# Eight LayerNorm tiles transposed by DMA in 16-bit halves instead of on TensorE

## The chip, the cores and the metric

One core of one Trainium2 chip. The metric is the device time of one execution in microseconds. A core has TensorE (PE, matmuls, results in PSUM), VectorE (DVE), ScalarE (ACT), GpSimd (POOL), and SyncE (SP), whose queue issues nearly all DMA transfers of this kernel. Each engine works through its own instructions in order; semaphores order the engines among themselves.

## The reference

A transformer block with adaptive LayerNorm: 2048 rows of 512 values, attention with 32 query heads over 8 cached key/value heads (the last 512 cached positions), and a gated feed-forward of width 1792.

```python
x = A_x
mod = (_silu(c) @ w_mod).reshape(c.shape[0], 6, 1, -1)
sa, ca, ga, sb, cb, gb = (mod[:, 0], mod[:, 1], mod[:, 2], mod[:, 3], mod[:, 4], mod[:, 5])
h = _layernorm(x, axis=-1) * (1 + ca) + sa
x = x + ga * _A_ref(h, A_k_cache, A_v_cache, A_wq, A_wo)   # softmax(q k^T / sqrt(128)) v, then wo
h = _layernorm(x, axis=-1) * (1 + cb) + sb                 # the second LayerNorm
x = x + gb * _B_ref(h, B_w_gate, B_w_up, B_w_down)         # (gelu(h wg) * (h wu)) wd
```

All tensors are float32. The kernel keeps precision by splitting each operand in two 16-bit halves, a high part and the remainder (a *pair*), and makes each product of three matmuls: low x high, high x high, high x low (`mm3`).

## The kernel before

**The stages.** The attention runs over 128 *units*: two halves of the rows (first 1024, last 1024), in each half 16 pairs of heads, in each pair two heads times two blocks of 512 rows. A unit is four *slots*; slot `t` handles 128 rows of one head: scores on PE (`ps`), row maximum on DVE (`nm`, L982), exponential on ACT (`ee`, L991), the high half of the probabilities on ACT two slots later (`p`, L1003), the low half on DVE three slots later (L1008), and then one DMA transpose of both halves (`pt`, L1012). The product of probabilities and values (`po`) of a unit is made two units later. Its results (`ot` pairs) wait for the output projection (`py`), which runs tile by tile over the next eight units, once four heads are there, and adds into `acc`, the residual rows. The scores have two PSUM banks, in turn; the other PSUM tiles share five under the tag `acc`.

**The order of the work** is written out by hand. In every slot the code issues the scores, the maximum, the delayed steps, then up to three product groups of `mm3` from a list (`pop()`: query projection, `py`, `po`), then whatever is registered for this slot: `at(t, fn)`, then the loads that fall due, and last `at(("w", t), fn)`. `spare` moves background transfers into slots that have no other.

**The second LayerNorm of the first 1024 rows.** When the last addition to a row tile of 128 rows is made (`attn_final`), `ln_tile(2, ...)` returns seven steps that are registered 1, 5, 8, 9, 10, 12 and 13 slots later: `stat` (mean and variance on DVE, a power on POOL), `norm` (POOL, in place in `acc`), `turn` (four transposes of 128x128 on PE against the identity, into a PSUM tile `pln`), two affine steps (ACT, `hf<-pln,cols`, after the second the result is written to DRAM as `hs`), and two steps that split the result into the pair blocks of the feed-forward stage (ACT high, POOL low). Twelve slots later the tile of `acc` is loaded with rows of the second half. There are eight such tiles, `ti` 0 to 7, around the change from the first to the second half of the attention. The tiles of `ln_tile(1, ...)`, the first LayerNorm of the last 1024 rows, use the same `turn` earlier on. The second LayerNorm of the last 1024 rows (`ln_turned`) already turns its tiles by DMA, in the feed-forward stage.

**In the same stretch** the modulation columns are made (`mod_col`, L137, which reads `sbc`, a tile of the tag `ot`), and the feed-forward weights begin to be prepared (`prep_set`), through tiles of the tag `raw` (`stage`), which five buffers serve and from which `hf` is taken too.

**The feed-forward stage** multiplies by a seven-product scheme (Strassen-like): from four blocks 11, 12, 21, 22 of the gated activations four combinations t1, t3, t2, t4 are made (`sums_of`), and all are kept as pairs `at`. For five passes of seven the down projection uses them (`turned(n)`), in the order of products 1, 2, 6, 5, 7, 3, 4; product 5 reads t1, 7 reads t3, 6 reads t2, 4 reads t4. The pairs `at` share the tag `ot` with the attention outputs.

Of the kernel before, what the change touches and what calls it, by code (L numbers as in the profile page):

```python
# [11 lines left out]
F16 = mybir.dt.float16  # L12
U16 = mybir.dt.uint16
BF16 = mybir.dt.bfloat16
AF = mybir.ActivationFunctionType
ALU = mybir.AluOpType
# [23 lines left out]
GU = 2.0 ** -38  # L40
PRE = 2.0 ** -20
TINY = 1e-36
NOT = 12
LDGAP = 1
NRAW = 5
NRW = 2
# [18 lines left out]
def block_kernel(ctx: ExitStack, tc: tile.TileContext, x, kT, v, wq, wo, wg, wu, wd, cT, wc, wm, out):  # L65
# [8 lines left out]
    def tmp(name):  # L74
        return pool.tile([P, 512], F32, tag="e", name=name, bufs=NE)

    def raw(name):
        return pool.tile([P, 512], F32, tag="raw", name=name, bufs=NRAW)
# [397 lines left out]
    def ln_tile(gen, i, src):  # L476
        jsc, jsh = ln_cols("a" if gen < 2 else "f")
        qb, i = divmod(i % (2 * QT), QT)
        st = {}

        def load():
            if gen == 2:
                st["x"] = src()
            else:
                st["x"] = raw("xs")
                dma(st["x"], src())

        def stat():
            ln_stat(st["x"], st)
            ln_power(st)  # L490

        def norm():
            if gen == 2:
                return pool_ts(st["x"], st["x"], st["mv"][:, 0:1], st["rs"], ALU.subtract, ALU.mult)
            nc.vector.tensor_scalar(st["x"], st["x"], st["mv"][:, 0:1], st["rs"], op0=ALU.subtract, op1=ALU.mult)

        def turn():
            st["ps"] = bank("acc", "pln", NACC)
            for dt in range(KT):
                nc.tensor.transpose(st["ps"][:, dt * P:(dt + 1) * P], st["x"][:, dt * P:(dt + 1) * P], ident)  # L500

        def affine(dts):
            if 0 in dts:
                st["f"] = raw("hf") if gen == 2 else tmp("hf")
            f = st["f"]
            for dt in dts:
                sl = slice(dt * P, (dt + 1) * P)
                nc.scalar.activation(f[:, sl], st["ps"][:, sl], AF.Identity,
                                     scale=cols[:, jsc, dt:dt + 1], bias=cols[:, jsh, dt:dt + 1])
            if KT - 1 in dts:  # L510
                dma(spilled(gen, qb)[:, :, i * P:(i + 1) * P], f.rearrange("p (k q) -> p k q", k=KT))

        def parts(act):
            o = slice(i * P, (i + 1) * P)
            f = st["f"].rearrange("p (k q) -> p k q", k=KT)
            for h, name in enumerate(("b11", "b21") if qb == 0 else (None, "b22")):
                if name:
                    t, src = block(gen, name), f[:, 2 * h:2 * h + 2, :]
                    if act:
                        nc.scalar.activation(t[:, 0:2, o], src, AF.Copy)  # L520
                    else:
                        nc.gpsimd.tensor_tensor(t[:, 2:4, o], src, t[:, 0:2, o], op=ALU.subtract)

        more = [lambda: parts(True), lambda: parts(False)]
        return load, [stat, norm, turn, lambda: affine((0, 1)), lambda: affine((2, 3))] + more

    TURN = {}

# [429 lines left out]
    def attn_final(ti):  # L958
        y1[ti] = dram.tile([P, D], F32, name=f"y{ti}")
        dma(y1[ti], acc[ti])  # L960
        if ti < 2 * QT:
            nxt = ti + 2 * QT
            own, steps = ln_tile(2, ti, lambda: acc[ti])
            own()
            for d, fn in zip((1, 5, 8, 9, 10, 12, 13), steps):
                at(("w", now[0] + d), fn)
            at(now[0] + 12, lambda: load_acc(nxt, rows_of(x, nxt)))
        else:
            ln_last(ti - 2 * QT)
# [294 lines left out]
    def f_items(q, hold=None):  # L1264
        n, m = divmod(q, 2)
        st = {}
        done = set()

        def add(k, src):
            nc.vector.tensor_tensor(st[k], st[k], st[src], op=ALU.add)  # L1270

        def gelu(key, src):

            def apply():
                dst = tmp("fg") if key == "21" else src
                nc.scalar.activation(dst, src, AF.Gelu_apprx_tanh, scale=col("finv", f_scale(q)))
                G[n, key] = dst

            return (apply,)

        def result(key, src):
            if m == 0:
                for step in gelu(key, src):
                    step()
            else:
                g = G[n, key]
                nc.vector.scalar_tensor_tensor(g, g, col("gsc", n % NP), src, op0=ALU.mult, op1=ALU.mult)  # L1287
                if not turned(n):
                    parts(key, G.pop((n, key)), nc.vector)
                elif key != "12":  # L1290
                    parts(key, g, nc.vector)
                else:
                    sums_of()

        def parts(key, g, eng):
            t = A[n, key] = pair("ot", "at", NOT)
            nc.scalar.activation(t[:, 0, :], g, AF.Copy)  # L1297
            eng.tensor_tensor(t[:, 1, :], g, t[:, 0, :], op=ALU.subtract)

        def sums_of():  # L1300
            g = {k: G.pop((n, k)) for k in ("11", "12", "21", "22")}
            for o, a, b in (("11", "12", "11"), ("12", "22", "12"), ("22", "22", "11"), ("21", "21", "22")):
                nc.gpsimd.tensor_tensor(g[o], g[a], g[b], op=ALU.subtract)  # L1303
                parts({"11": "t1", "12": "t3", "22": "t2", "21": "t4"}[o], g[o], nc.gpsimd)

        def out_(key, src):
            if not hold:
                result(key, src)
            else:
                hold.append(gelu(key, src))  # L1310

        def place(k):
            if m == 0:
                return pool.tile([P, QB], F32, tag="k", name="fg", bufs=2) if k == 6 else tmp("fg")
            return pool.tile([P, QB], F32, tag="p16", name="fu", bufs=NP16) if k == "s1" else kept(k)

        def after(k):
            done.add(k)
            if k in (1, 6, 7):
                name = {1: "s1", 6: "u2", 7: "u3"}[k]  # L1320
                keep(st, name, place(name))
            if k == 2:
                add("s1", "b")
                out_("11", st["s1"])
            elif k == 4:
                out_("21", st["a"])
            elif k == 3:
                add("u2", "c")
                out_("12", st["u2"])
            if k in (5, 7) and {5, 7} <= done:  # L1330
                add("u3", "c")
                out_("22", st["u3"])

        tags = {"a": ("s", "fa", 2) if q else ("qa", "fa", 1), "b": ("acc", "fb", NACC), "c": ("acc", "fc", NACC)}
        return with_posts(("f", q), 2 + q // (2 * NP), banks(st, tags), after)
# [448 lines left out]
```

## Time and profile before

| what | value |
|---|---|
| three runs | 1743.76, 1745.96, 1745.58 us; median 1745.58 |
| profiled execution | 1743.57 us, with a span of 1741.8 us |
| granted TensorE clock | 1.0 |
| busy: PE, DVE, ACT, POOL | 1714.7, 1417.6, 1258.5, 1045.9 us |
| DMA | 339.82 MB, mean 195 GB/s |

The span is the time from the first to the last instruction of the profiled execution. Busy time is what the profiler saw an engine work; a share of it is an average over stages with different limits. In a row of the timeline the first number is the start in us from the span's start, the second the length; the releaser in brackets is what ended the engine's idle time by the semaphores of the profile, and where an instruction waits for several, it may name the wrong one. In a row of a group the numbers behind the bar are busy us and mean ns of one; in a row of one tile or source line the three numbers are the shortest, median and longest in ns.

### The profile page before, as it was taken

Reading aid. Unit: us, or ns where it says so; the run is one execution under the profiler, and the core shown is the slowest. Engines: PE = TensorE matmul, PEld = TensorE weight load, DVE = VectorE, ACT = ScalarE, POOL = GpSimd, SP = SyncE. Lnnn points to the kernel's source line nnn. Section 1 sums busy time; section 2 is a strip of 40 time slices with the busy share of each in tenths; the row PEclk is TensorE's granted clock in tenths of the full one; section 3 lists DMA queues with packets and bytes.
Section 4 is the critical chain, followed back from the end, with each engine's and each line's share of the span. In section 5 each row is a group of like instructions: output and inputs, shape, how many; then the busy total and the mean of one; then the engine's idle time right before and its main releaser. Section 6 shows DMA issues by size and latency. Waiting matters only on the chain.

```text
span 1741.8 us, 26188 instructions
## 1 busy us (share of the span) xinstructions
PE 1714.7 (98%) x8022; PEld 787.0 (45%) x8022; DVE 1417.6 (81%) x2454; ACT 1258.5 (72%) x2813; POOL 1045.9 (60%) x1266
## 2 busy tenths in 40 slices
PE   7999999999999999999999999999999999999998
PEld 5444444444444444444444444444444444444443
DVE  7898898888888899888888788888886678556674
ACT  6988788888878777898778778787784554643344
POOL 4889778776788884654675665754621558313422
PEclk9999999999999999999999999999999999999999
DMA  7999999999999999999999999899986663743235
GB/s 236 218 205 211 213 214 207 223 206 221 215 217 228 205 205 187 212 213 230 201 219 224 208 223 220 186 235 218 197 180 150 187 177 128 191 139 100 91 97 167
DMA packets 690636, 339.82 MB, mean 195 GB/s; under 512 B 578880, under 2 KB 601408, under 8 KB 690496
## 3 DMA queue, kind: packets, MB, share of 16 engines
q1 hardware_dynamic: 690208, 337.63, 85.5%
q8 instruction: 63, 1.03, 0.3%
q14 instruction: 77, 0.63, 0.1%
q10 hardware_dynamic: 288, 0.52, 0.1%
HBM read 135.66 MB, written 61.87 MB: 113 GB/s over the span
## 4 chain that ended last, share of the span: by engine, by line
PE 82%; ACT 5%; DVE 5%; DMA 3%; POOL 2%; issue 2%; SPq 0%; ACTq 0%; DVEq 0%; POOLq 0%
PE py L90 19%; PE ps L90 17%; PE po L90 17%; PE qa L90 8%; PE fa L90 6%; PE qc L90 4%; PE fc L90 3%; PE ya L90 2%; PE qb L90 2%; PE fb L90 2%; PE yc L90 1%; ACT ee L991 1%; DMA yv<-yu 1%; ACT p L1003 1%; DVE nm L982 1%
## 5 line engine op out<-in xcount | busy, mean ns | idle before, releaser
L991 ACT ACTIVATE ee<-ps,nm 128x512 f32<-128x512 f32 x512 | 350.1, 684 | 191.9 <-DVE nm L982 189.3
L1008 DVE SCALAR_TENSOR_TENSOR p<-ee,rr,p 128x512 f16<-128x512 f32 x512 | 460.0, 898 | 4.5 <-ACT p L1003 3.9
L982 DVE TENSOR_REDUCE nm<-ps 128x1 f32<-128x512 f32 x512 | 350.4, 684 | 106.1 <-PE ps L90 103.2
L90 PE MATMUL ps<-k,qt 128*128 128x512 f16 x1536 | 414.9, 379 | 5.6 <-ACT ee L991 4.4
L1003 ACT ACTIVATE p<-ee,rr 128x512 f16<-128x512 f32 x512 | 364.6, 712 | 19.0 <-DVE rr L999 10.0
L90 PE MATMUL po<-pt,v 128*128 128x512 f16 x1536 | 373.0, 379 | 2.7 <-DVE kmax L183 1.4
L90 PE MATMUL py<-wo,ot 128*128 128x512 f16 x1536 | 371.5, 379 | 0.1
L90 PEld LDWEIGHTS <-w 128*128 128x128 f16 x2184 | 213.3, 98 | 263.3 <-issue 4.7
L90 PEld LDWEIGHTS <-v 128*128 128x128 f16 x1536 | 149.9, 98 | 184.9 <-DMA pt<-p 2.3
L90 PEld LDWEIGHTS <-ot 128*128 128x128 f16 x1536 | 150.3, 98 | 181.7 <-DVE ot L740 0.5
L90 PEld LDWEIGHTS <-qt 128*128 128x128 f16 x1536 | 145.9, 98 | 176.9 <-issue 4.7
L1303 POOL TENSOR_TENSOR fg<-fg 128x512 f32<-128x512 f32 x40 | 51.8, 1295 | 135.6 <-DVE fg L1287 103.0
L740 DVE SCALAR_TENSOR_TENSOR ot<-po,ot 128x512 f16<-128x512 f32 x128 | 87.7, 685 | 39.1 <-ACT ot L739 38.6
L1297 ACT ACTIVATE at<-fg 128x512 f16<-128x512 f32 x86 | 53.4, 625 | 64.8 <-DVE fg L1287 44.5
L991 ACT ACTIVATION_READ_ACCUMULATOR ee<-ps,nm 128x1 f32 x512 | 99.9, 195 | 0.0
L952 DVE SCALAR_TENSOR_TENSOR acc<-py,ysc,acc 128x512 f32<-128x512 f32 x128 | 94.7, 740 | 6.2 <-PE py L90 6.2
L235 POOL TENSOR_TENSOR lw<-lw,half__86 128x1 f32<-128x1 f32 x37 | 23.4, 633 | 104.2 <-DVE lw L185 104.1
L90 PE MATMUL fa<-t,w 128*128 128x512 f16 x336 | 83.6, 379 | 1.9 <-ACT u L885 1.4
L90 PE MATMUL qa<-t,w 128*128 128x512 f16 x348 | 84.9, 379 | 0.0
L397 POOL TENSOR_TENSOR rs<-rs,nhalf 128x1 f32<-128x1 f32 x32 | 18.8, 586 | 103.6 <-DVE rs L391 100.7
L739 ACT ACTIVATE ot<-po 128x512 f16<-128x512 f32 x128 | 73.8, 577 | 5.0 <-PE po L90 5.0
L1657 DVE SCALAR_TENSOR_TENSOR yt<-ya,dyc,yt 128x512 f32<-128x512 f32 x68 | 50.1, 745 | 22.1 <-PE ya L90 21.7
(241 smaller groups left out, 2794.0 us busy)
## 6 DMA issues: line engine op xcount, KB each, us to landing
w<-kept SPq DMA_DIRECT2D x123, 256.0 KB, 3.3
wo<-kept SPq DMA_DIRECT2D x70, 256.0 KB, 3.4
kept<-stage SPq DMA_DIRECT2D x61, 256.0 KB, 3.3
raw<-in_wo SPq DMA_DIRECT2D x56, 256.0 KB, 3.2
kept<-w SPq DMA_DIRECT2D x39, 256.0 KB, 3.4
rw<-in_wq SPq DMA_DIRECT2D x38, 256.0 KB, 3.2
hs<-hf SPq DMA_DIRECT2D x32, 256.0 KB, 2.9
pt<-p SPq DMA_TRANSPOSE x512, 3.5
```

Of the source, the lines that this page charges most:

```text
L90: nc.tensor.matmul(ps, a, b, start=first and n == 0, stop=last and n == 2, skip_group_check=chain)
L235: nc.gpsimd.tensor_tensor(out, out, half_, op=ALU.pow)
L739: nc.scalar.activation(t[:, 0, :], src, AF.Copy, scale=scale)
L740: return lambda: nc.vector.scalar_tensor_tensor(t[:, 1, :], src, scale, t[:, 0, :], op0=ALU.mult, op1=ALU.subtract)
L952: nc.vector.scalar_tensor_tensor(acc[ti], st["p"], by, acc[ti], op0=ALU.mult, op1=ALU.add)
L982: nc.vector.tensor_reduce(nm, E[t]["ps"], axis=AX.X, op=ALU.max, negate=True)
L991: nc.scalar.activation(e, E[t]["ps"], AF.Exp, bias=E[t]["nm"], scale=1.0, accum_out=sm[:, t % 2:t % 2 + 1])
L1003: nc.scalar.activation(p16[:, 0, :], E[t]["e"], AF.Copy, scale=E[t]["r"])
L1008: nc.vector.scalar_tensor_tensor(p16[:, 1, :], E[t]["e"], E[t]["r"], p16[:, 0, :], op0=ALU.mult, op1=ALU.subtract)
L1297: nc.scalar.activation(t[:, 0, :], g, AF.Copy)
L1303: nc.gpsimd.tensor_tensor(g[o], g[a], g[b], op=ALU.subtract)
L1657: nc.vector.scalar_tensor_tensor(YT[key], ps, by, YT[key], op0=ALU.mult, op1=ALU.add)
```

## The change

For the eight tiles of the second LayerNorm of the first 1024 rows, the four PE transposes are replaced by: a copy to the high 16-bit half on ACT (`high`), the remainder on POOL (`low`), one DMA transpose of both halves (`turn_dma`, in SP's queue), and the sum of the two turned halves on DVE into a tile `hf` of the tag `raw` (`joined`). The affine steps then work in place in that tile. The steps stand 1, 5, 8, 9, 12, 16, 18, 19, 21 and 22 slots behind the last addition. The halves take a new tag `lnh` of three buffers, the turned halves `lnt` of two. In the feed-forward stage the combinations t1, t3 and t2 now take `lnh` and t4 takes `lnt`, and the tag `ot` has 10 buffers instead of 12. The tiles of `ln_tile(1, ...)` keep the PE transposes.

```diff
--- before.py
+++ after.py
@@ -40,7 +40,7 @@
 GU = 2.0 ** -38
 PRE = 2.0 ** -20
 TINY = 1e-36
-NOT = 12
+NOT = 10
 LDGAP = 1
 NRAW = 5
 NRW = 2
@@ -499,9 +499,25 @@
             for dt in range(KT):
                 nc.tensor.transpose(st["ps"][:, dt * P:(dt + 1) * P], st["x"][:, dt * P:(dt + 1) * P], ident)
 
+        def high():
+            st["h"] = pair("lnh", "lnh", 3)
+            nc.scalar.activation(st["h"][:, 0, :], st["x"], AF.Copy)
+
+        def low():
+            nc.gpsimd.tensor_tensor(st["h"][:, 1, :], st["x"], st["h"][:, 0, :], op=ALU.subtract)
+
+        def turn_dma():
+            st["t"] = pool.tile([P, 2, KT, P], F16, tag="lnt", name="lnt", bufs=2)
+            nc.sync.dma_start_transpose(st["t"].rearrange("p h k q -> p (h k) q"), st["h"].rearrange("p a b -> p (a b)"))
+
+        def joined():
+            st["f"] = raw("hf")
+            nc.vector.tensor_tensor(st["f"].rearrange("p (k q) -> p k q", k=KT), st["t"][:, 0], st["t"][:, 1], op=ALU.add)
+            st["ps"] = st["f"]
+
         def affine(dts):
-            if 0 in dts:
-                st["f"] = raw("hf") if gen == 2 else tmp("hf")
+            if 0 in dts and gen < 2:
+                st["f"] = tmp("hf")
             f = st["f"]
             for dt in dts:
                 sl = slice(dt * P, (dt + 1) * P)
@@ -522,7 +538,8 @@
                         nc.gpsimd.tensor_tensor(t[:, 2:4, o], src, t[:, 0:2, o], op=ALU.subtract)
 
         more = [lambda: parts(True), lambda: parts(False)]
-        return load, [stat, norm, turn, lambda: affine((0, 1)), lambda: affine((2, 3))] + more
+        turns = [high, low, turn_dma, joined] if gen == 2 else [turn]
+        return load, [stat, norm] + turns + [lambda: affine((0, 1)), lambda: affine((2, 3))] + more
 
     TURN = {}
 
@@ -962,7 +979,7 @@
             nxt = ti + 2 * QT
             own, steps = ln_tile(2, ti, lambda: acc[ti])
             own()
-            for d, fn in zip((1, 5, 8, 9, 10, 12, 13), steps):
+            for d, fn in zip((1, 5, 8, 9, 12, 16, 18, 19, 21, 22), steps):
                 at(("w", now[0] + d), fn)
             at(now[0] + 12, lambda: load_acc(nxt, rows_of(x, nxt)))
         else:
@@ -1293,7 +1310,7 @@
                     sums_of()
 
         def parts(key, g, eng):
-            t = A[n, key] = pair("ot", "at", NOT)
+            t = A[n, key] = pair(*{"t4": ("lnt", "at", 2)}.get(key, ("lnh", "at", 3) if key[0] == "t" else ("ot", "at", NOT)))
             nc.scalar.activation(t[:, 0, :], g, AF.Copy)
             eng.tensor_tensor(t[:, 1, :], g, t[:, 0, :], op=ALU.subtract)
 
```

## The prediction

> **What bounds the kernel now.** I read the page first, for the engine that has no room, then the page's chain that ended last.
>
> ```profile
> span 1741.8 us, 26188 instructions
> PE 1714.7 (98%) x8022; PEld 787.0 (45%) x8022; DVE 1417.6 (81%) x2454; ACT 1258.5 (72%) x2813; POOL 1045.9 (60%) x1266
> PE 82%; ACT 5%; DVE 5%; DMA 3%; POOL 2%; issue 2%; SPq 0%; ACTq 0%; DVEq 0%; POOLq 0%
> ```
>
> TensorE (PE) is busy 98% of the span and carries 82% of the chain. A microsecond taken from PE is a microsecond off the end, unless another engine becomes the limit in that stretch. So the next views are PE's own timeline around the eight turns, and the busy times by stretch there.
>
> ```profile
> L500 PE MATMUL pln<-ident,acc x32: 272/273/300, 700.4 to 775.5; 128*128 128x128 f32 x32
> 699.75 0.81 PE L90 MATMUL po<-pt,v 128*128 128x512 f16 x3
> 700.39 0.60 PE L500 MATMUL pln<-ident,acc 128*128 128x128 f32 x4
> 700.83 0.81 PE L90 MATMUL ps<-k,qt 128*128 128x512 f16 x3
> ...
> 730.84 0.81 PE L90 MATMUL po<-pt,v 128*128 128x512 f16 x3
> 732.28 0.63 PE L500 MATMUL pln<-ident,acc 128*128 128x128 f32 x4 [0.63 <-POOL w L158]
> ...
> 774.02 0.81 PE L90 MATMUL po<-pt,v 128*128 128x512 f16 x3
> 775.15 0.63 PE L500 MATMUL pln<-ident,acc 128*128 128x128 f32 x4 [0.33 <-ACT hf L508]
> ```
>
> ```profile
> 540.00:550.00 10.00, 8.56 (x41) 3.77 (x40) 9.41 (x16) 8.57 (x22) 7.35 (x9) 1.00 1.20 226
> 700.00:780.00 80.00, 79.04 (x385) 37.96 (x384) 69.98 (x134) 69.17 (x172) 45.79 (x50) 1.00 1.00 212
> 720.00:760.00 40.00, 39.37 (x191) 18.74 (x190) 37.74 (x73) 34.25 (x86) 27.13 (x27) 1.00 0.99 213
> 700.00:800.00 100.00, 99.04 (x478) 47.01 (x477) 86.55 (x162) 85.78 (x212) 53.57 (x58) 1.00 0.99 213
> ```
>
> The columns of the second fence are PE, weight load, DVE (VectorE), ACT, POOL, granted clock, DMA share and GB/s. From 700 to 780 PE idles 0.96 us of 80, and both waits that this consists of stand before a turn. DVE is the next engine: 94% between 720 and 760.
>
> **What goes.** Starts, not lengths, give PE's cost, because matmuls overlap: three matmuls take 700.39 - 699.75 = 0.64 us, and the four transposes of a tile 700.83 - 700.39 = 0.44 us. Eight tiles give 3.5 us. Two turns also began late: 732.28 - 730.84 - 0.64 = 0.80 us and 775.15 - 774.02 - 0.64 = 0.49 us. The first is put down to POOL, but it ends 0.14 us after this ACT group, which read the previous tile's `pln` bank:
>
> ```profile
> 731.34 0.80 ACT L508 ACTIVATE hf<-pln,cols 128x128 f32<-128x128 f32 x2
> ```
>
> These are the two places where tiles follow each other by three slots instead of four or five. I read both waits as waits for a PSUM bank; with `pln` gone for these tiles the bank is not asked for. Together 3.5 + 1.3 = 4.8 us leave PE. No larger gain is in reach: PE's other idle time lies outside this stretch.
>
> **What comes.** Each of the eight tiles gets one ACT copy (`high`), one POOL subtraction (`low`), one DMA transpose of 128x1024 16-bit values, one DVE sum (`joined`). The nearest rows, by instruction and shape:
>
> ```profile
> L1297 ACT ACTIVATE at<-fg 128x512 f16<-128x512 f32 x86 | 53.4, 625 | 64.8 <-DVE fg L1287 44.5
> L508 ACT ACTIVATE hf<-pln,cols 128x128 f32<-128x128 f32 x32 | 12.9, 458 | 0.0
> L520 ACT ACTIVATE b<-hf 128x256 f16<-128x256 f32 x12 | 4.5, 404 | 0.0
> L159 POOL TENSOR_TENSOR w<-rw,w 128x512 f16<-128x512 f32 x4 | 6.0, 1509 | 0.3
> L449 DVE TENSOR_TENSOR b<-hf,b x3: 678/679/680, 20.6 to 40.4; 128x512 f16<-128x512 f32 x3
> L1008 DVE SCALAR_TENSOR_TENSOR p<-ee,rr,p 128x512 f16<-128x512 f32 x42 | 34.9, 831 | 1.8 <-ACT p L1003 1.8
> L1008 DVE SCALAR_TENSOR_TENSOR p<-ee,rr,p x42: 725/743/1671, 691.0 to 798.4; 128x512 f16<-128x512 f32 x42
> L1012 SPq DMA_TRANSPOSE pt<-p x40: 1231/1247/2662, 691.8 to 798.1; - x40
> DMA to landing us min/median/max: 3.0/3.5/5.3
> ```
>
> *ACT.* Eight copies at 0.625 = 5.0 us. The affine steps read SBUF instead of PSUM: 0.458 us at the most, and a twice wider read of SBUF takes 0.404, so 32 times 0 to -0.05 us. ACT idles 10.8 us between 700 and 780, and the affine steps and parts of the later tiles move beyond 780, so I cost this at nothing. Without that cover it would be up to 5 us. `high` stands in the slot where the turn stood and waits for the same POOL normalisation, three slots earlier; behind it on ACT queue the exponentials.
>
> *DVE.* Eight sums at 0.68 = 5.4 us, in a place that matters. A turn comes every (775.15 - 700.39)/7 = 10.7 us. A slot is 2.59 us (728.90 - 726.31, below), and `joined` sits eight slots, 20.7 us, behind the old turn: at 721, 732, 742, 753 and on to 796. So four sums, 2.7 us, fall between 720 and 760. POOL's work also stretches DVE's: L1008 has a median of 743 ns and a mean of 831, so 42 x 0.088 = 3.7 us of stretch beside 53.57 us of POOL, 0.07 per us; four more subtractions of 1.5 us add 0.4 us. DVE then asks for 37.74 + 2.7 + 0.4 = 40.8 us in a stretch that PE would cross in 40 - 4 x 0.44 - 0.80 = 37.4 us. DVE is the slower by 3.4 us. (The Trainium skill, GPSIMD Engine Reference, section Key points, says that POOL shares its SBUF interfaces with DVE and contends with DVE instructions that have two SBUF inputs, which `joined` has; the 743 to 831 ns agree, and a `joined` stretched as L1008 at its worst would add 0.9 us to one sum.)
>
> How far DVE may fall behind before PE stalls is seen here (scores `ps`, their maximum `nm`, the exponential `ee`; PE has two `ps` banks):
>
> ```profile
> 723.72 0.81 PE L90 MATMUL ps<-k,qt 128*128 128x512 f16 x3
> 726.31 0.81 PE L90 MATMUL ps<-k,qt 128*128 128x512 f16 x3
> 726.44 0.68 DVE L982 TENSOR_REDUCE nm<-ps 128x1 f32<-128x512 f32 x1
> 727.16 0.69 ACT L991 ACTIVATE ee<-ps,nm 128x512 f32<-128x512 f32 x1 [0.72 <-DVE nm L982]
> 727.75 0.19 ACT L991 ACTIVATION_READ_ACCUMULATOR ee<-ps,nm 128x1 f32 x1
> 728.90 0.81 PE L90 MATMUL ps<-k,qt 128*128 128x512 f16 x3
> ```
>
> The scores of 723.72 ended at 724.53, DVE took them 1.9 us late, ACT released the bank at 727.94, and PE wanted it at 728.90: 1.0 us was left, so a lag of 2.9 us is free. Of the 3.4 us that leaves 0.5 us of PE stall if DVE never idles; it idled 2.3 us there before, some of that in waits on ACT that stay. Bounds 0 and 3.4 us; I take 1.0, near the lower end, because most of that idle time is fillable.
>
> *The `raw` buffers.* `joined` takes one of five, and each is held from step 16 to 22 instead of 9 to 13: two tiles at once. Near the end the weight preparation takes four:
>
> ```profile
> 784.43 0.43 SPq L96 DMA_DIRECT2D kept<-stage  x1
> 787.60 0.62 POOL L158 TENSOR_SCALAR stage<-rw 128x512 f16<-128x512 f32 x1 [3.58 <-DMA kept<-stage]
> 788.30 1.16 POOL L159 TENSOR_TENSOR stage<-rw,stage 128x512 f16<-128x512 f32 x1
> 789.90 0.52 SPq L96 DMA_DIRECT2D kept<-stage  x1
> ```
>
> POOL waits 3.58 us for such a buffer already. Tile 7's `joined` falls due about 787, when the five hold two `hf` and three or four `stage`. The next is free at about 791 (POOL's split of tile 5, behind 788.30 + 1.16) or 793 (the store of 789.90 plus a landing). Then DVE, with all `nm` queued behind it, waits 4 to 6 us, of which 2.9 are free: 1.1 to 3.1 us of stall, or nothing if a buffer comes free earlier. I take 0.6, near the lower end, as it may strike once.
>
> *POOL and SP.* Eight subtractions of 1.2 to 1.5 us fit in POOL's idle time (45.79 busy of 80). Two SP steps newly wait for them: the transpose, three slots later, and the reload of `acc`, at step 12, which waited for PE's turn before; behind each in SP's queue stand the `pt` transposes that feed PE. Three slots are 7.8 us, so nothing; if POOL is later than that, SP stands still for the rest. A transpose occupies SP 1.23 us and pushes `pt` back by that, and the DMA engines by one landing of 3.5 us. I cost that at nothing here and price it as a rival. The spill and the splits of a tile come nine slots later; their reader is the feed-forward stage, hundreds of microseconds away: nothing.
>
> *The other buffers.* `ot` falls from 12 to 10. By program order at most nine output pairs live at once, with `sbc` ten, and a pair written in a unit reuses one whose last `py` read stands four groups (2.6 us) earlier on PE: nothing. In the feed-forward stage t1, t3, t2 have one set of three instead of a share of twelve; their last reads of the pass before (products 5, 7, 6) stand on PE ahead of the product whose result writes them: nothing. Without that cover, one product of three matmuls, 0.64 us, in each of eight passes, 5.1 us.
>
> **Sum.** -4.8 + 1.0 + 0.6 = -3.2 us. The profiled execution took 1743.57 us with its span of 1741.8 us, so it would be 1740.4; the median of the runs shown, 1745.58, lies 2.0 us higher, and the same sum makes it 1742.4. The bound of 0.2% is 3.5 us, close to this.
>
> **Rivals.**
>
> *Everything is covered.* DVE's idle time takes the sums and a buffer is free for tile 7: -4.8 us, 1740.8. For it: DVE lagged 1.9 us without a PE wait. Against: 3.4 us over in 40.
>
> *DVE and the buffers take it all.* Stall at the upper ends, 3.4 + 3.1 = 6.5: +1.7 us, 1747.3. For it: the crowding at 787. Against: both at their worst.
>
> *The transposes delay `pt` (slower).* The added transposes go through the queue and the DMA engines that feed PE, at a DMA share of 1.00 between 700 and 780. What a jam costs was seen once, at a share of 1.20:
>
> ```profile
> 540.71 3.72 SPq L1012 DMA_TRANSPOSE pt<-p  x1
> 547.92 2.10 PE L90 MATMUL po<-pt,v 128*128 128x512 f16 x9 [1.44 <-DVE kmax L183]
> ```
>
> The issue took 3.72 us instead of 1.23, and PE stood 1.44 us before the `po` that reads such a `pt` (the DVE instruction named has nothing to do with `po`, so I read it as the transfer). If each added transpose did that, 8 x 1.44 = 11.5 us on the forecast, +8.3, 1753.9; from five of the eight on (7.2 - 3.2 = 4.0) the change is slower beyond the bound. Against it: `pt` has four slots, 10.4 us, and 40 transposes around here land within 5.3 us. (The Trainium skill, VectorE: DVE Perf Modes, section The three transpose paths, speaks against the change too: 1309 ns for a 128x128 16-bit block by DMA against 390 ns on TensorE, and in its rules TensorE where PSUM will do. By that figure a tile's eight blocks would take 10.5 us of DMA, an estimate; here a transpose of that size lands in 3.5 us, so the trace does not agree.)
>
> *The buffers do not cover.* The 5.1 us above on the forecast: +1.9, 1747.5; with waits at `ot` as well, more. For it: single buffers where there was slack. Against: the order on PE.
>
> **How the numbers follow.** Forecast 0.40, its own range -4.8 to -1.5, 1740.8 to 1744.1: 0.15 of it beyond the 3.5 us, 0.25 within. All covered 0.25, faster. All taken 0.12, same. `pt` delayed 0.17, slower. Buffers 0.06: 0.02 same, 0.04 slower. So faster 0.40, same 0.39, slower 0.21. The range reaches from 1739.5 (all covered, with the 1.1 us by which single runs lie off the middle) to 1750.5 (the delay at five to six tiles); what lies beyond is about half of that rival and little else.
>
> **What would show it.** Right: no `pln` on PE between 700 and 780, no PE wait of 0.8 and 0.5 at its place, `nm` lagging up to 2.9 us between 720 and 760, at most one DVE wait before a `joined`. Wrong: PE waits before `po` put down to `pt` or to its neighbours, SP standing before the new transpose, ACT waiting in `high`, an `at` or `ot` write waiting for PE in the feed-forward stage, or a PE stall of more than 2 us beside tile 7.

## The result and the profile after

The changed kernel takes 1754.17 us (median of 4 runs, 1751.99 to 1755.43), beside 1744.77 us for the kernel before (4 runs, 1743.76 to 1745.96): a ratio of 1.0054, 95% interval 1.0041 to 1.0067. The forecast was 3.2 us faster; it is 9.4 us slower. The profiled execution took 1754.54 us. Source lines below `joined` now have numbers 17 higher: `nm` is L999, `ee` L1008, the probabilities' low half L1025, `pt` L1029.

The page of the kernel after:

```profile
span 1752.7 us, 26131 instructions
PE 1714.8 (98%) x7988; PEld 784.5 (45%) x7990; DVE 1422.5 (81%) x2462; ACT 1263.5 (72%) x2821; POOL 1056.9 (60%) x1274
```

PE has 34 fewer matmul records (the 32 transposes are gone), the same share, and a span that is 10.9 us longer. The totals don't tell why; the stretch around the tiles does. Windows of the kernel after (from:to, length, PE, weight load, DVE, ACT, POOL, granted clock, DMA share, GB/s):

```profile
720.00:760.00 40.00, 36.63 (x168) 16.17 (x167) 37.86 (x72) 33.03 (x80) 30.31 (x27) 1.00 1.03 216
700.00:800.00 100.00, 90.41 (x415) 40.23 (x412) 87.40 (x160) 81.46 (x197) 66.36 (x63) 1.00 0.96 206
800.00:805.00 5.00, 3.84 (x10) 1.35 (x11) 2.80 (x5) 2.89 (x8) 0.00 (x0) 0.50 1.08 257
```

Between 700 and 800 PE had idled 0.96 us; now it idles 9.6, and then works five microseconds at half its clock. DVE between 720 and 760 is as busy as before (37.86 against 37.74 of 40): it did not fill its gaps with the sums. What PE waited for from 684 to 830, first before, then after (engine, line, releaser: total us, times, longest):

```profile
PE pln L500 <- POOL w L158: 0.6, 1, 0.6
PE pln L500 <- ACT hf L508: 0.3, 1, 0.3
```

```profile
PE ps L90 <- ACT ee L1008: 7.5, 8, 3.0
PE po L90 <- issue: 2.1, 1, 2.1
PE qa L90 <- ACT u L902: 1.0, 1, 1.0
```

The two bank waits before `pln` are gone; 10.6 us of other waits stand in their place. A stopwatch that does not depend on where the span starts: PE makes a few small products `pst` and `prow` at fixed places of the program. Three such rows before, then after:

```profile
684.64 0.38 PE L196 MATMUL pst<-ident,mm 128*128 128x128 f32 x2
764.70 0.60 PE L149 MATMUL prow<-ident,cols 128*128 128x128 f32 x4
818.38 0.17 PE L222 MATMUL pst<-lm,ones 128*128 128x2 bf16 x1
```

```profile
683.68 0.38 PE L196 MATMUL pst<-ident,mm 128*128 128x128 f32 x2
764.50 0.60 PE L149 MATMUL prow<-ident,cols 128*128 128x128 f32 x4
827.45 0.17 PE L222 MATMUL pst<-lm,ones 128*128 128x2 bf16 x1
```

Before, PE needs 80.06 us from the first mark to the second and 133.74 to the third; after, 80.82 and 143.77. So +0.8 and +10.0: the whole loss lies in these 134 us, and net of what the missing transposes give, nearly all of it behind the second mark. I use this stopwatch for every experiment; the change's own median stands beside it.

The worst place is the seventh tile (`ti` 6; the prediction and the first expectations count from one and call it tile 7), at its step `joined`:

```profile
789.86 0.81 PE L90 MATMUL ps<-k,qt 128*128 128x512 f16 x3
793.09 0.62 POOL L158 TENSOR_SCALAR stage<-rw 128x512 f16<-128x512 f32 x1 [4.07 <-DMA kept<-stage]
794.90 1.29 POOL L538 TENSOR_TENSOR b<-hf,b 128x256 f16<-128x256 f32 x2
795.60 1.14 DVE L515 TENSOR_TENSOR hf<-lnt 128x512 f32<-128x512 f16 x1 [2.60 <-POOL b L538]
796.67 0.68 DVE L999 TENSOR_REDUCE nm<-ps 128x1 f32<-128x512 f32 x1
797.38 0.69 ACT L1008 ACTIVATE ee<-ps,nm 128x512 f32<-128x512 f32 x1 [3.55 <-DVE nm L999]
798.21 0.81 PE L90 MATMUL ps<-k,qt 128*128 128x512 f16 x3 [3.01 <-ACT ee L1008]
801.16 4.00 PE L90 MATMUL po<-pt,v 128*128 128x512 f16 x9 [2.15 <-issue]
```

Read from the second row: POOL waits 4.07 us for a `raw` buffer (a store has to land first), so it splits an earlier tile's `hf` late, so the sum waits 2.60 us for the buffer that this split frees. All `nm` are queued behind the sum; ScalarE waits 3.55 us for the next, which belongs to the scores of the first row, and PE 3.01. Then PE waits 2.15 us more before `po`, and the nine matmuls, 2.10 us elsewhere, take 4.00 at the granted clock of 0.50.

### The profile page after: what moved, and what is told of

Read it like the earlier page. It is cut to its first block, busy times and chain, and to the rows that moved or that the text cites. A ratio compares the mean times of both kernels' runs of the same rounds, so it can differ in the third digit from the quotient of the medians.

```text
span 1752.7 us, 26131 instructions
## 1 busy us (share of the span) xinstructions
PE 1714.8 (98%) x7988; PEld 784.5 (45%) x7990; DVE 1422.5 (81%) x2462; ACT 1263.5 (72%) x2821; POOL 1056.9 (60%) x1274
## 4 chain that ended last, share of the span: by engine, by line
PE 82%; ACT 5%; POOL 4%; DVE 4%; DMA 3%; issue 2%; SPq 0%; POOLq 0%; ACTq 0%; DVEq 0%
PE py L90 19%; PE po L90 17%; PE ps L90 17%; PE qa L90 8%; PE fa L90 6%; PE qc L90 4%; PE fc L90 3%; PE ya L90 2%; PE qb L90 2%; PE fb L90 2%; PE yc L90 1%; ACT ee L1008 1%; ACT p L1020 1%; PE pq L90 1%; DMA yv<-yu 1%
## 5 line engine op out<-in xcount | busy, mean ns | idle before, releaser
L1008 ACT ACTIVATE ee<-ps,nm 128x512 f32<-128x512 f32 x512 | 349.6, 683 | 199.4 <-DVE nm L999 194.6
L1025 DVE SCALAR_TENSOR_TENSOR p<-ee,rr,p 128x512 f16<-128x512 f32 x512 | 460.3, 899 | 5.4 <-ACT p L1020 5.0
L999 DVE TENSOR_REDUCE nm<-ps 128x1 f32<-128x512 f32 x512 | 350.4, 684 | 101.6 <-PE ps L90 98.9
L1008 ACT ACTIVATION_READ_ACCUMULATOR ee<-ps,nm 128x1 f32 x512 | 99.8, 195 | 0.0
```

The costliest lines, as they stand in the source:

```text
L999: nc.vector.tensor_reduce(nm, E[t]["ps"], axis=AX.X, op=ALU.max, negate=True)
L1008: nc.scalar.activation(e, E[t]["ps"], AF.Exp, bias=E[t]["nm"], scale=1.0, accum_out=sm[:, t % 2:t % 2 + 1])
L1025: nc.vector.scalar_tensor_tensor(p16[:, 1, :], E[t]["e"], E[t]["r"], p16[:, 0, :], op0=ALU.mult, op1=ALU.subtract)
```

## The experiments

Three questions were asked of them: what the buffer costs, what the four added instructions cost, and why. `raw6` below means this edit, which adds a sixth `raw` buffer and pays for it with one `ot` buffer (in the kernel before it needs the new tags, and comes with the changed buffers for the combinations):

```diff
-NOT = 10
+NOT = 9
-        return pool.tile([P, 512], F32, tag="raw", name=name, bufs=NRAW)
+        return pool.tile([P, 512], F32, tag="raw", name=name, bufs=NRAW + 1)
-    sbc = pool.tile([P, D], F32, tag="ot", name="sbc", bufs=NOT)
+    sbc = pool.tile([P, D], F32, tag="lnh", name="sbc", bufs=3)
-            box["t"] = pool.tile([P, 2, 512], F16, tag="raw", name="stage", bufs=NRAW)
+            box["t"] = pool.tile([P, 2, 512], F16, tag="raw", name="stage", bufs=NRAW + 1)
```

All of them in one table; the last columns are the stopwatch, us more than before at the second and the third mark (from one profile each). The kernel before was run along with each group, with medians of 1744.2 to 1744.8.

| kernel | median us | ratio to before, interval | 2nd | 3rd |
|---|---|---|---|---|
| changed | 1754.2 | 1.0054 (1.0041 to 1.0067) | +0.8 | +10.0 |
| changed, raw6 | 1750.1 | 1.0034 (1.0022 to 1.0046) | +0.9 | +5.5 |
| before with the changed buffers for combinations | 1744.6 | 1.0003 (0.9994 to 1.0013) | 0.0 | +0.7 |
| changed, no sums | 1751.2 | 1.0041 (1.0026 to 1.0056) | -1.5 | +6.4 |
| changed, sums on POOL | 1753.9 | 1.0056 (1.0039 to 1.0072) | +0.9 | +8.7 |
| changed, raw6, no sums | 1745.5 | 1.0005 (0.9995 to 1.0014) | -1.6 | +1.6 |
| changed, raw6, no ACT copies | 1753.6 | 1.0052 (1.0038 to 1.0067) | +1.8 | +6.7 |
| changed, raw6, neither | 1746.9 | 1.0015 (1.0005 to 1.0024) | -2.3 | +0.2 |
| halves and transposes added, turn stays on PE | 1746.9 | 1.0013 (1.0004 to 1.0022) | 0.0 | +2.1 |
| first four tiles by DMA | 1746.5 | 1.0011 (1.0002 to 1.0020) | +0.5 | +5.1 |
| tiles 4 to 6 by DMA, raw6 | 1747.4 | 1.0015 (1.0007 to 1.0024) | -0.9 | +4.0 |
| last four by DMA, raw6 | 1743.1 | 0.9991 (0.9982 to 0.9999) | -1.0 | -0.1 |
| before, raw6 | 1745.6 | 1.0004 (0.9995 to 1.0013) | -0.1 | -0.1 |
| changed, raw6, narrow columns | 1748.7 | 1.0023 (1.0013 to 1.0033) | -0.2 | +3.7 |
| before, raw6, narrow columns | 1743.8 | 0.9996 (0.9987 to 1.0005) | -0.5 | -0.9 |

The four kernels with a later weight preparation have a table of their own below. Between the third mark and the end, single profiles differ by some 2 us in either direction, and some profiled runs lie that far from their median (the kernel with neither 2.9 us below it); where a median and a stopwatch disagree by that much I trust neither to tell less.

**The buffer and the sums, one at a time.** Four kernels: the changed one with `raw6`; before with only the new buffers (`NOT = 10`, t1 to t3 in `lnh`, t4 in `lnt`); the changed one without the sums; the same with the sums on POOL.

```diff
-            nc.vector.tensor_tensor(st["f"].rearrange("p (k q) -> p k q", k=KT), st["t"][:, 0], st["t"][:, 1], op=ALU.add)
-            st["ps"] = st["f"]
+            st["ps"] = st["t"][:, 0].rearrange("p k q -> p (k q)")
```

The fourth keeps both lines that the third replaces, with `nc.gpsimd` for `nc.vector` in the first of them.

> The changed kernel with a sixth raw buffer (paid for by moving sbc to the tag lnh and taking ot from 10 to 9). Theory A, the raw buffer: in the changed kernel DVE waits 2.60 us for a buffer before tile 7's sum, PE then idles 3.01 us, and its granted clock falls to 0.50 between 800 and 805; by the start times of the row maxima against the kernel before, the lag grows there from 3.3 to 9.1 us. Without that wait the time falls by 5.8 us, to about 1748.4, with no clock drop near 800. Theory B, VectorE and ScalarE late between 720 and 780 (waits of PE of 5.3 us): the wait is only the last of a row and another takes its place: less than 2 us gained, above 1752. Theory C, the new buffers of the combinations: no change here, 1754.

> The kernel before with the buffers of the combinations alone (ot 10, t1, t2, t3 from lnh, t4 from lnt); the LayerNorm as before. Theory C: the lag that the changed kernel gains after 1340 us, about 2.5 us, comes from these buffers: 1747.3. Theories A and B: it does not; 1744.8, within 1 us of the kernel before.

> The changed kernel without the eight sums on VectorE: the affine steps read the turned high half, and the raw buffer is taken by the first affine step, two slots later; the low half is left out of the result. Theory B: the PE waits between 720 and 790 (5.3 us) go, and theory A: the buffer is held for four slots instead of six and ScalarE, not VectorE, would wait for it: with both, 10 us less, 1744; with B alone 1749; if the added ScalarE, POOL and DMA work is the cause rather than the sum, PE still waits 3 us or more between 720 and 780.

> The changed kernel with the eight sums on POOL instead of VectorE. Theory B, in which VectorE's own time is short: PE waits between 720 and 780 shrink from 5.3 us to under 2, and POOL instead of VectorE waits for the raw buffer of tile 7, behind which no row maximum stands: 1744 to 1747. Rival: POOL is as late as VectorE was (19.4 us busy of 20 between 720 and 740), so that splits, transposes and weights come late and PE waits for these: 1752 or more.

The sixth buffer takes 4.1 us off (1754.2 to 1750.1) and 4.5 on the stopwatch: the 3.01 us stall and the half clock are gone. Between 5 and 6 us are left. The combinations' buffers cost nothing that can be measured. Without the sums PE is 1.5 us ahead at the second mark where the changed kernel is 0.8 behind. It then stands 5.92 us one tile earlier, at the sixth: ScalarE's affine step now waits there for a `raw` buffer. So buffer and sums are two separate costs, and taking one out alone shows the other. POOL as the place for the sums gains nothing (1753.9): PE's waits before scores fall from 7.5 to 3.7 us, but the one before `po` grows from 2.1 to 4.9.

**What is left without the buffer's wait.** Sixth buffer and no sums; sixth buffer and no `high` on ScalarE (the normalisation on POOL writes the high half, the low half is that of other values, and the result is not exact); neither sums nor `high`; and a kernel in which PE keeps the turn and the halves and their transposes are only added.

```diff
-                return pool_ts(st["x"], st["x"], st["mv"][:, 0:1], st["rs"], ALU.subtract, ALU.mult)
+                st["h"] = pair("lnh", "lnh", 3)
+                return pool_ts(st["h"][:, 0, :], st["x"], st["mv"][:, 0:1], st["rs"], ALU.subtract, ALU.mult)
...
-        turns = [high, low, turn_dma, joined] if gen == 2 else [turn]
+        turns = [turn, high, low, turn_dma] if gen == 2 else [turn]
```

> The changed kernel with a sixth raw buffer and without the eight sums on DVE (the affine steps read the turned high half; the low half is left out of the result). Three theories share out the 5.9 us that are left between the sixth-buffer kernel (1750.1) and before (1744.2), less the 2 us that taking the turns off PE gives. If the sums alone cost it (S), nothing is lost once they are gone: the lag behind before stays at -2 from slot 279 on, 1742. If ScalarE's eight copies and later affine steps cost another 2.5 to 3 us in slots 289 to 297 (H), the lag goes from -2.2 to about +0.6 there and stays, 1744.8. If the transposes and their reads cost it (P), the sums make no difference and it stays at 1750.

> The changed kernel with a sixth raw buffer and without ScalarE's eight copies: the normalisation on POOL writes the 16-bit high half itself, the residue that POOL subtracts is then that of other values (result not kept exact). By H (ScalarE late in slots 289 to 297 for its 8 x 0.63 us more) the wait before the query projection on ACT u and those before ps on ACT ee shrink and it comes to 1747.3, 2.8 below the sixth-buffer kernel's 1750.1. By S (only the sums on DVE) nothing changes, 1750.1. By P nothing changes either.

> Sixth raw buffer, no sums on DVE, no copies on ScalarE; the POOL subtractions, the DMA transposes and the affine steps from SBUF stay. If S and H are all, the lag ends at -2 to -3: 1741.5 to 1742.2. If what is lost in slots 289 to 297 has another cause (the affine steps and splits of the last tiles moved later, the transposes in SP's queue), it ends as the kernel without sums alone, at about 1744.8.

> The changed kernel, but PE keeps its turn and the affine steps read PSUM at the old slots; ACT's copy, POOL's subtraction and the DMA transpose are made and not used, no sum. So it is before plus three of the four additions and no gain. If they are free, as I costed them: 1744.2. By H the eight copies cost about 2.5 to 3 with the rest in its old place: 1747. By P (transposes in the queue that feeds PE) up to 1755.7, with PE waits before po.

The sums cost 4.6 us (1750.1 to 1745.5; 3.9 on the stopwatch). H fell as the main cause: without ScalarE's copies the kernel is not faster but slower, and in the last kernel of the four, which has them all, PE loses nothing up to the second mark. There copies, subtractions and transposes were free. The slower one (1753.6) loses 1.2 us more on the stopwatch than with the copies; 0.9 of it stand at the second mark already, where the cause is not settled, and behind it the clock drops (see the last section). A small share of H stays open: without sums, leaving the copies out as well puts PE 0.8 us further ahead at the second mark, while the median gets worse. P holds at one place only. PE's waits from 684 to 830 in the kernel with the sixth buffer and no sums, then in the one that keeps the turn:

```profile
PE po L90 <- issue: 2.1, 1, 2.1
PE ps L90 <- ACT ee L1007: 1.6, 4, 0.6
PE qa L90 <- ACT u L901: 1.3, 2, 1.0
```

```profile
PE pln L500 <- ACT hf L519: 1.5, 2, 0.9
PE po L90 <- DMA pt<-p: 1.2, 2, 0.9
```

The `po` is the same in both, that of slot 302, and it waits in nearly every variant. Its rows before, then in the kernel that keeps the turn:

```profile
790.52 1.31 SPq L1012 DMA_TRANSPOSE pt<-p  x1
794.39 2.11 PE L90 MATMUL po<-pt,v 128*128 128x512 f16 x9
```

```profile
788.41 1.47 POOL L159 TENSOR_TENSOR stage<-rw,stage 128x512 f16<-128x512 f32 x1
789.91 0.34 SPq L96 DMA_DIRECT2D rw<-in_wu  x1
790.31 0.61 SPq L96 DMA_DIRECT2D kept<-stage  x1
791.03 1.29 SPq L1024 DMA_TRANSPOSE pt<-p  x1
795.25 2.10 PE L90 MATMUL po<-pt,v 128*128 128x512 f16 x9 [0.92 <-DMA pt<-p]
```

SP stands until POOL has made a `stage`, issues a load and a store, and only then the `pt` that PE needs. Before, that `pt` was issued 3.87 us ahead of its reader, about one landing (median 3.8 us between 776 and 805): just in time. Counted from the first mark, POOL's `stage` is done 1.2 us later than before and this `pt` is issued 1.3 us later. So with the weight preparation in its place, what PE gains ahead of slot 302 is taken back here, and what makes POOL later is added.

**The weight preparation moved away.** Twelve slots later (`b = T // 2 + 42 + 26 * n` for `b = T // 2 + 30 + 27 * n`): in before, in the changed kernel, without sums, and with only the last four tiles by DMA (five `raw` buffers in all).

> The kernel before with the weight preparation twelve slots later (first set from slot 298 instead of 286, each period 26 slots instead of 27). A control for the next three. Q (a pt transpose that waits in SP's queue behind POOL's stage sets PE's earliest po at slot 302, just in time before): nothing to gain here, 1744.4. If the move does harm of its own, it is seen here.

> The changed kernel with the weight preparation twelve slots later, so that tile 7's joined finds a raw buffer with five, and no load or store of a stage stands in SP's queue ahead of the pt of slot 302. Raw buffers (3.6 us by the sixth-buffer kernel) and Q (2.1 us before that po) both right: 1754.2 - 5.7 = 1748.5. Raw buffers only, the pt being late by the added transposes themselves (P): 1750.5. The sums' cost stays in either case.

> The changed kernel without the sums on DVE and with the weight preparation twelve slots later. With sixth buffer and no sums it came to 1745.5 with 2.06 us of PE wait before the po of slot 302. By Q that wait goes: 1743.4, and the lag of -2 to -3 us of slot 287 is kept. By P it stays, 1745.5.

> The weight preparation twelve slots later, and only the last four tiles turned by DMA with the sums (slots 290 to 302, behind the modulation columns), the first four by PE. D1 (a sum costs only where VectorE is full, 720 to 760): 4 x 0.44 + 0.5 off, nothing on, 1742.0. D2 (each sum costs about its own 0.6 us wherever it stands ahead of a row maximum in VectorE's queue): 2.3 off, 2.4 on, 1744.3.

| preparation later | median us | ratio to before, interval | to the last `pst` of its stretch, us | PE waits 684 to 830 |
|---|---|---|---|---|
| before | 1753.2 | 1.0051 (1.0036 to 1.0066) | 143.44 | 0.5 |
| changed | 1755.2 | 1.0061 (1.0043 to 1.0078) | 144.60 | 4.3 |
| no sums | 1752.2 | 1.0041 (1.0025 to 1.0057) | 141.58 | 1.7 |
| last four by DMA | 1750.5 | 1.0031 (1.0017 to 1.0045) | 141.89 | 0.6 |

The move itself costs 8.8 us, most of it later, between 880 and 1100, where PE now idles 7.6 us, and puts all four medians far above what was expected; only differences to the first row count (the last `pst` here is another one than in the table above). The intervals of the four overlap, so the medians hardly tell them apart, and what follows rests on one profile each. In this company the change costs 1.2 us on the stopwatch instead of 10, and no `po` waits, nor any sum for a buffer. The transposes are all still there, so they alone don't delay `po`; Q and the buffer fit. The move doesn't prove them one by one, since it also takes POOL's work on the weights away (18.4 us busy between 780 and 830 instead of 25.9). Without sums it gains 1.9, with the last four tiles alone 1.6.

**Which sums.** First four tiles alone (their sums at slots 274 to 286); tiles 4 to 6 and tiles 4 to 7, with `raw6` (here the numbers are `ti`, counted from 0); and before with `raw6` as control. In the first, `i < 4`:

```diff
-        turns = [high, low, turn_dma, joined] if gen == 2 else [turn]
+        turns = [high, low, turn_dma, joined] if gen == 2 and i < 4 else [turn]
-            for d, fn in zip((1, 5, 8, 9, 12, 16, 18, 19, 21, 22), steps):
+            for d, fn in zip((1, 5, 8, 9, 12, 16, 18, 19, 21, 22) if ti < 4 else (1, 5, 8, 9, 10, 12, 13), steps):
```

> Only the first four tiles turned by DMA (their sums at slots 274 to 286, among the modulation columns), the last four by PE; weight preparation and five raw buffers as in the changed kernel. D1 (a sum costs where VectorE is full): the lag rises by about 3 us between slots 273 and 289 as with all eight, less what the four turns give, and nothing strikes later: 1746.5. D2 (every sum costs about its 0.6 us): 2.4 on, 2.3 off, 1744.3.

> Only tiles 4 to 6 turned by DMA, a sixth raw buffer, the preparation in its old place. D1: the sums stand where VectorE has room, 3 x 0.44 + 0.8 = 2.1 us off by slot 300, of which the pt transpose of slot 302, which waits for POOL's stages, takes back what PE is early: 1743.0 to 1744.4. D2: 1744.5 to 1746.

> As the last, with tile 7 as well. Against its own control the same four tiles with the preparation twelve slots later gave 2.7 us. D1 with the wait at slot 302: 1743.0 to 1744.8. D2: 1744.5 to 1746. If the sixth buffer lets POOL make its stages earlier, the wait before that po shrinks and it beats before by up to 2.5: 1742.

> Control: before, with the changed kernel's buffers for the combinations and a sixth raw buffer. POOL's 3.58 us wait for a stage buffer goes; if PE depends on it (Q), little: before shows no PE wait between 780 and 800, so 1744.4 by every theory. Anything else would be the effect of the buffer alone.

The first four alone make the kernel slower (1746.5, as D1 had it; 5.1 us on the stopwatch), the last four don't (1743.1, within D1's range). But D1 also said that nothing strikes later, and the trace has 4.6 of the 5.1 us behind the second mark, with 1.4 us before a `pln` and 1.2 before `po` among its waits. The variant with tiles 4 to 6 missed its range (1747.4): its sum for `ti` 6 waited 1.01 us for a `raw` buffer in spite of the sixth, and the PE wait that followed cost it, together with the `po` of slot 302, a clock drop, below. The kernel with the last four is 0.1% faster than before, which the interval only just tells from nothing; and as the stopwatch shows no gain there (-0.1), I can't say that it comes from the turns.

**VectorE relieved.** The four modulation columns that stand among the first four sums are cut to an eighth of their width (the rest is left out of the result), in the changed kernel with `raw6` and in its control.

```diff
-        nc.vector.scalar_tensor_tensor(src, src, 1.0, by, op0=ALU.mult, op1=ALU.mult, accum_out=c)
+        w = slice(0, 64 if j == 5 else D)
+        nc.vector.scalar_tensor_tensor(src[:, w], src[:, w], 1.0, by[:, w], op0=ALU.mult, op1=ALU.mult, accum_out=c)
```

> The sixth-buffer kernel with all eight sums, and VectorE relieved in the same stretch: the four modulation columns at slots 274 to 286 take 64 of 512 elements each (the rest of those sums is left out of the result), some 0.5 us less each, 2 us. D1 (the sums cost because VectorE has no room between 720 and 760): 2 to 3 us come back, 1747 to 1748. D3 (the first four sums cost because of where they stand ahead of a row maximum, whatever else VectorE has to do): 1750.1 as before.

> Control: the same narrow columns in before with the sixth buffer. Before shows no PE wait for VectorE there, so 1744.5 to 1745.6, no change, by every theory.

1.4 us come back (1750.1 to 1748.7; 1.8 on the stopwatch), less than D1's 2 to 3, and the intervals overlap. The control, expected to stay, gets faster about as much (1745.6 to 1743.8; 0.74 on the stopwatch, against 1.78). So the medians leave nothing for VectorE's load ahead of the sums, and the stopwatch 1.0 us: the first PE wait falls from 1.28 to 0.32 us, the others stay. That it is a part of the cause rests on this one wait. How a sum comes to delay PE is to be seen in the row order there, in the changed kernel with `raw6`, and below it the same slot in the kernel before:

```profile
729.51 0.81 PE L90 MATMUL ps<-k,qt 128*128 128x512 f16 x3
732.41 1.72 POOL L159 TENSOR_TENSOR w<-rw,w 128x512 f16<-128x512 f32 x1
732.43 0.67 DVE L137 SCALAR_TENSOR_TENSOR wmc<-wmc,sbc 128x512 f32<-128x512 f32 x1
733.04 1.63 DVE L515 TENSOR_TENSOR hf<-lnt 128x512 f32<-128x512 f16 x1
734.08 1.60 POOL L507 TENSOR_TENSOR lnh<-acc,lnh 128x512 f16<-128x512 f32 x1
734.59 0.68 DVE L999 TENSOR_REDUCE nm<-ps 128x1 f32<-128x512 f32 x1
735.31 0.69 ACT L1008 ACTIVATE ee<-ps,nm 128x512 f32<-128x512 f32 x1 [1.98 <-DVE nm L999]
736.14 0.81 PE L90 MATMUL ps<-k,qt 128*128 128x512 f16 x3 [1.28 <-ACT ee L1008]
```

```profile
732.75 0.81 PE L90 MATMUL ps<-k,qt 128*128 128x512 f16 x3
734.45 0.68 DVE L982 TENSOR_REDUCE nm<-ps 128x1 f32<-128x512 f32 x1
```

The scores that ended at 730.32 are taken at 734.59, 4.3 us late. The sum is the last of the instructions ahead of the maximum: 1.63 us instead of 0.68, while POOL runs one subtraction and then the next. Before, the scores of this slot ended at 733.56 and were taken 0.9 us late. Counted from the first mark, PE is 2.5 us earlier now and the maximum 0.9 us later: most of the lag is PE's own gain, which a DVE with hardly any idle time does not follow. ScalarE frees the bank at 736.08, and PE has lost 1.28 us, so 3.0 us of lag were free here.

## Why the prediction was wrong

*PE's gain: mechanism right, worth less than half.* No `pln` is left between 700 and 780, and both bank waits are gone. But the 4.8 us don't arrive. With sums and preparation out of the way the gain is 1.9 us (in one profile). ScalarE then ends the waits (`ps` on `ee`, `qa` on `u`, 1.7 us in that kernel; 2.9 with the preparation in its old place). The prediction looked for the next limit on DVE alone; PE's was the first of several that lay close together.

*The sums: the term that failed.* I took 1.0 us, with an upper bound of 3.4. They cost 4.6 (3.9 on the stopwatch). Three steps were wrong. The instruction: eight sums were priced at 0.68 us; in the changed kernel with the sixth buffer they take

```profile
L515 DVE TENSOR_TENSOR hf<-lnt 128x512 f32<-128x512 f16 x8 | 6.6, 824 | 0.8 <-DMA lnt<-lnh 0.8
```

The 0.9 us by which one might be stretched were named and left out of the sum; one was (1.63). Then the idle time: DVE's 2.3 us of idle time in 720 to 760 were called fillable, and 2.1 of them are still there after. Last, only the four sums between 720 and 760 were costed. By the kernels with the sixth buffer, with sums and without, 2.5 us are lost up to the second mark, within the bound, and 1.4 behind it, where the working has nothing. The free lag of 2.9 us was right (3.0 at the first wait).

*The `raw` buffers: mechanism right, 0.6 us put for 4.1.* The wait, its place and the buffer are as described. That the stall lies in its range (1.1 to 3.1 forecast, 3.01 measured) is luck: DVE waited 2.60 us, not 4 to 6, but the scores ended at 790.67 and would have been taken 3.4 us late even without that wait, so of the 2.9 free us none was left. I took the low end because it strikes once, and I did not price what follows a stall: the half clock that makes the next `po` 1.9 us longer.

*ACT, POOL, SP, DMA at nothing: right up to slot 291*, by the kernel that only adds them, and the added transposes land in nearly the usual time (median 4.1 us, longest 5.7). Behind it they cost 2.1 us, 1.2 of it in waits before `po`, most at one `pt` that was just in time. The rival of the delayed `pt` had the right victim and the wrong cause: no jam of transposes, but SP's order behind POOL. Its figure for all eight tiles, 1753.9, lies beside the measured 1754.2 by chance. I had followed the queue for the step that was moved, and not looked for a `pt` whose issue already hung on POOL. One reading was off without visible harm: the affine steps from SBUF take 0.48 us, not 0.46 at the most.

*The other buffers: right* (1.0003).

*Which signs showed it.* Of those given ahead for a wrong forecast two came, the stall of more than 2 us beside tile 7 and a wait before `po`; of those for a right one `nm`'s lag went past its 2.9 us, and a second `joined` waited too, for its transpose (0.8 us). By its mechanism it came nearest to the rival in which DVE and the buffers take it all; its +1.7 us had both at the upper bounds, and both bounds were too low.

*The sum again.* With -1.9 for the transposes, 4.6 for the sums, 4.1 for the buffer and 2.1 for what was put at nothing, it comes to +8.9 of the 9.4 us measured. The four come from different pairs of kernels and need not add up, so this is a tally and no proof. (The lower end of the range should read 1739.7, 1740.8 less 1.1; nothing hangs on it.)

## What to carry to other kernels

An instruction added to an in-order queue costs its length at the place where the next critical instruction stands behind it; look up the lag there, slot by slot, and price it at the length that it has beside the other engines' work. Time that the busiest engine gains is itself lag for the engine that it waits for. A tile held longer has to be counted against everything that shares its buffers at the end of its life, and a buffer wait ahead of a critical instruction is paid by the whole chain and can be paid again by the clock. Ask also which transfers are only just in time: a gain on the busiest engine ends at the first of them.

## What the runs showed of the hardware

Idle time drops PE's clock here, and it need not be one long gap. In the changed kernel gaps of 3.01 and 2.15 us with 0.8 us of work between them gave 0.50 from 800 to 805; the product between the two still took 0.81 us, as elsewhere. In the variant with tiles 4 to 6 it took less (first PE's rows, then the windows):

```profile
794.48 0.81 PE L90 MATMUL ps<-k,qt 128*128 128x512 f16 x3 [1.76 <-ACT ee L1009]
796.70 3.62 PE L90 MATMUL po<-pt,v 128*128 128x512 f16 x9 [1.41 <-DMA pt<-p]
```

```profile
795.00:800.00 5.00, 3.59 (x11) 1.24 (x10) 3.37 (x6) 4.05 (x12) 0.00 (x0) 0.66 1.06 234
```

Less still in the kernel with the sixth buffer and no copies on ScalarE, where the `po` takes 3.49 us instead of 2.10:

```profile
796.03 0.81 PE L90 MATMUL ps<-k,qt 128*128 128x512 f16 x3 [0.32 <-ACT ee L1008]
799.08 3.49 PE L90 MATMUL po<-pt,v 128*128 128x512 f16 x9 [2.24 <-issue]
```

A single gap of 2.06 us before the same `po` (sixth buffer, no sums) left the clock at 1.00; the single gap of 5.92 us (no sums, five buffers) did not:

```profile
785.00:790.00 5.00, 0.00 (x0) 0.00 (x0) 0.00 (x0) 1.34 (x3) 3.33 (x4) 0.64 0.91 191
```

The Trainium skill, TensorE: Matmul & The Clock Gate, section Why this matters for your kernels, asks for no PE-idle gap over about 3 us between bursts. The gap of 5.92 us agrees with that; but gaps of 1.76 and 1.41 us, or of 0.32 and 2.24, none of them near 3, were enough together, and here the measurement decides.

POOL stretches a DVE sum of two SBUF tiles to 1.63 us from 0.68 while it runs a subtraction of two tiles of its own; these are the longest and the shortest of the same eight instructions, of one shape, in one kernel. Beside a POOL instruction with one input tile the sum stayed at 0.68 us (the changed kernel's third sum, beside a TENSOR_SCALAR of 128x512).
